# Second-layer weights as four neighbouring rows per partition, and last stores of 3, 6, 9 and 9 rows

## The chip, the cores and the metric

The kernel runs on one NeuronCore of one Trainium2 chip. The metric is the device time of one execution in microseconds (us). Before the change the median of three runs is 207.63 us (207.09 to 207.95).

## What is computed

Per batch and head (8 x 8, 576 positions, 64 dimensions) an attention over 32 pooled memory slots, and then a soft mixture of 8 experts over all 4608 rows of 512. The change touches only the experts and the output:

```python
    logits = x @ phi                       # x: 4608 x 512, phi: 512 x 32
    slot_input = d.T @ x                   # d: softmax of the logits over the rows
    for e in range(E):                     # 8 experts, 4 slots each
        h = np.maximum(slot_input[e] @ w1[e], 0.0)   # w1[e]: 512 x 1024
        slot_out[e] = h @ w2[e]                      # w2[e]: 1024 x 512
    return c @ slot_out                    # c: softmax of the logits over the 32 slots
```

All data are float32 in DRAM: 38 MB of q, k, v, 4.7 MB of phi, 16.8 MB each of w1 and w2, and an output of 9.4 MB.

## The kernel before, in words

The kernel writes no instruction directly. Each step is handed to a planner (`Plan.add`, L46) with its engine, a cost and the tiles that it reads and writes. The planner plays the program through with these costs and sets the order on each engine (`Plan.order`, L79). Loads and stores all go through the DMA queue of SyncE (SP), in planned order; each waits until the space that it fills, or the data that it sends, is free or ready.

The attention of the four pairs of batches runs first. Weights are loaded beside it, one half of a w1 matrix or of a w2 matrix (1 MB) at a time, into 20 slots of 2048 floats per partition (`ws`, L1258) and two more (`wqs`, L1260). A w1 half lands as two rows of 1024 floats per partition.

`expert_in` (L1323) is the first layer. For each expert and each half it issues 8 matmuls (L1332): the expert's 4 slots, with neighbours a weight block of 128 x 32, stand still, and 256 of the 1024 hidden units move through. The quarter `j` of the units goes to column tile `j` of TensorE (PE), so that quarter `j` of the hidden units ends on partitions 32j to 32j + 31 of the accumulator `hb`. `hidden` (L1343) applies the ReLU, splitting even and odd columns of `hb` apart, transposes both and scatters them to `hT`. So `hT` holds at partition p the units 256 j + 2 p + t, for j in 0 to 3 and t in 0 to 1.

`expert_out` (L1370) is the second layer. It needs row 256 j + 2 p + t of w2 at partition p, and so loads w2 as two neighbouring rows per partition and quarter: 256 contiguous pieces of 4 KB in each 1 MB load. Each half takes 16 matmuls of 128 x 32 by 256 (L1383), 8 for each half of the output columns, into `kvbank` and `scbank`. The very last megabyte is loaded in four parts of 256 KB (pieces of 1 KB).

Then `slot_sums` (L1304) copies both accumulators and adds the column tiles by matmul (L1316); L1499 and L1504 split the sums in two parts for the float32r format, and `out_mult` (L1510) multiplies the 32 slot outputs with the weights `c`. An output row here is one position of 9 per partition: the output is seen as 4 blocks `bp` of 128 partitions x 9 rows of 512. Each row of a block is a matmul pair (L1513), a copy from its accumulator bank by ScalarE (L1566) or VectorE (L1568) in turn, and its share of a store. The first three rows are stored one by one (L1546), the other 33 in 11 stores of three neighbouring rows (L1576): 6 KB in one piece per partition. They share 6 output tiles (`ots`, L1259), which lie over the weight slots, so a copy can have to wait for an earlier store.

Of the kernel before, what the change touches and what calls it, by code (L numbers as in the profile page):

```python
# [16 lines left out]
PE, DVE, ACT, POOL, SP = range(5)  # L17
# [3 lines left out]
class Plan:  # L21
# [24 lines left out]
    def add(self, eng, cost, fn, r=(), w=(), also=(), pri=None, dma=0.0, slack=0.0):  # L46
        cost, ni = cost if isinstance(cost, tuple) else (cost, 4)
        i = len(self.ops)
        deps = set()
        tiles = {}  # L50
        for x in r:
            for key in x:
                tiles[key[0]] = None
                if key in self.last_w:
                    deps.add(self.last_w[key])
        for x in w:
            for key in x:
                tiles[key[0]] = None
                if key in self.last_w:
                    deps.add(self.last_w[key])  # L60
                deps.update(self.reads.get(key, ()))
        for x in w:
            for key in x:
                self.last_w[key] = i
                self.reads[key] = []
        for x in r:
            for key in x:
                self.reads.setdefault(key, []).append(i)
        deps.discard(i)
        tiles = [t for t in tiles if t.pool is not None]  # L70
        for t in tiles:
            t.users += 1
        need = tiles + [t for t in also if t not in tiles]
        if pri is None:
            pri = self.phase[0]
            self.phase[0] += self.phase[1]
        self.ops.append((eng, cost, fn, deps, pri, dma, tiles, need, slack, ni))
# [170 lines left out]
def dve(n):  # L248
    return 0.15 + n / 960.0


def act(n, psum=True):
    return (0.16 if psum else 0.19) + n / 1200.0
# [15 lines left out]
def kernel(  # L269
# [24 lines left out]
    nc = tc.nc  # L294
    B, H, S, D = q.shape
    M = phi.shape[3]
    E, DM, FF = w1.shape
# [69 lines left out]
    def area(off, shape, n, below=(), fifo=False):  # L367

        size = shaped(off, shape)[1][1]
        xs = [shaped(off + i * size, shape) for i in range(n)]  # L370
        return Slots([a for a, _ in xs], [r for _, r in xs], below, fifo)
# [79 lines left out]
    def f():  # L451
        nc.vector.memset(ones, 1.0)
        for a in kps.aps:
            nc.vector.memset(a, 0.0)
        for a in sexs.aps:
            nc.vector.memset(a[:, PC:], 1.0)
        nc.vector.tensor_reduce(
            maskhp, ident.rearrange("p (c x) -> p c x", c=2), axis=AX.X, op=ALU.add
        )
        nc.vector.tensor_reduce(  # L460
            maskc, ident.rearrange("p (c x) -> p c x", c=C), axis=AX.X, op=ALU.add
        )
        nc.vector.tensor_reduce(
            rep[:, 0, :], ident.rearrange("p (a m) -> p m a", a=4), axis=AX.X, op=ALU.add
        )
        nc.vector.tensor_copy(rep[:, 1:4, :], rep[:, 0:1, :].to_broadcast([P, 3, NS]))
# [779 lines left out]
    def over(shape, n):  # L1246
# [10 lines left out]
    W0 = ARENA - NW * W_SZ  # L1257
    ws = area(W0, [W_SZ], NW, early)  # L1258
    ots = area(W0, [OT_SZ], NOUT, [ws])  # L1259
    wqs = Slots(  # L1260
        [qtile[:, i * W_SZ: i * W_SZ + W_SZ] for i in range(2)],
        [(TOP + i * W_SZ, W_SZ) for i in range(2)], [qs],
# [60 lines left out]
    def expert_in(e, hb):  # L1323
        w1v = w1[e].rearrange("(c p) f -> p c f", p=P)
        w1b = [load_w(w1v[:, 2 * i: 2 * i + 2], wqs if e == EG else ws) for i in range(2)]
        for i in range(2):

            def f(i=i):
                wv = w1b[i].ap.rearrange("p (c f) -> p c f", c=2)
                for c in range(2):  # L1330
                    for j in range(4):
                        nc.tensor.matmul(  # L1332
                            hb.ap[NS * j: NS * j + NS, :256],
                            SIM.ap[:, 2 * i + c, NS * e: NS * e + NS],
                            wv[:, c, 256 * j: 256 * j + 256],
                            start=(e % EG == 0 and i == 0 and c == 0),
                            stop=(e % EG == EG - 1 and i == 1 and c == 1),
                            tile_position=(0, NS * j),
                        )

            add(PE, (0.9, 32), f, r=[SIM, w1b[i]], w=[hb])
# [26 lines left out]
        )  # L1368

    def expert_out(e):  # L1370
        w2v = w2[e].rearrange("(j p t) d -> p j (t d)", j=4, t=2)
        w2h = w2[e].rearrange("(j p t) d -> p j t d", j=4, t=2)
        for i in range(2):
            last = e == E - 1 and i == 1
            t = ws.tile()
            wide = lambda t=t: t.ap.rearrange("p (j t d) -> p j t d", j=2, t=2)

            def mult(dst, d0, n, start, stop, i=i, wide=wide):
                for t in range(2):
                    for j in range(2):  # L1380

                        x = 2 * t + j
                        nc.tensor.matmul(  # L1383
                            dst[NS * x: NS * x + NS, :n],
                            hT()[:, 4 * t + 2 * i + j, NS * e: NS * e + NS],
                            wide()[:, j, t, d0: d0 + n],
                            start=start,
                            stop=stop,
                            tile_position=(0, NS * x),
                        )  # L1390

            if not last:
                load(
                    lambda t=t: t.ap.rearrange("p (a x) -> p a x", a=2),
                    w2v[:, 2 * i: 2 * i + 2], 1 << 20, t,
                )
                for d in range(2):
                    add(
                        PE, (0.5, 16),
                        lambda d=d, mult=mult, i=i: mult(  # L1400
                            pacc[d].ap[:, 0], d * HD, HD, e == 0 and i == 0, False
                        ),
                        r=[hTb.part(e // EG), t], w=[pacc[d]],
                    )
                continue
            t.split(4)
            for d in range(2):
                for j in range(2):
                    load(
                        lambda d=d, j=j: wide()[:, j, :, d * HD: d * HD + HD],  # L1410
                        w2h[:, 2 * i + j, :, d * HD: d * HD + HD], 1 << 18, t.part(2 * d + j),
                    )
            for d in range(2):
                add(
                    PE, (0.5, 16), lambda d=d, mult=mult: mult(pacc[d].ap[:, 0], d * HD, HD, False, True),
                    r=[hTb.part(e // EG), t.part(2 * d), t.part(2 * d + 1)], w=[pacc[d]],
                )
# [92 lines left out]
    def out_mult(bp, j, po, x):  # L1510
        y = HALF * (j % 2)
        for t in range(2):
            nc.tensor.matmul(  # L1513
                po.ap[:, : x.stop - x.start],
                cT[bp].ap[y: y + HALF, j // 2 * P: j // 2 * P + P],
                sr.ap[y: y + HALF, t, x],
                start=(t == 0),
                stop=(t == 1),
                tile_position=(y, 0),
            )  # L1520

    ot0 = ots.tile().split(2 * G)
    for d in range(2):
        x = slice(d * HD, d * HD + HD)
        for i in range(G):
# [17 lines left out]
            if d == 1:  # L1543
# [4 lines left out]
                    ),  # L1548
                    r=[ot0.part(2 * i), ot0.part(2 * i + 1)], dma=P * DM * 4 / DMA_RATE,
                )  # L1550
    for bp in range(NBP):
        for j0 in range(0 if bp else G, J, G):
            ot = ots.tile().split(G)
            for i in range(G):
                t = bp * J + j0 + i
                po = b_o.tile()
                add(
                    PE, 0.43,
                    lambda po=po, i=i, bp=bp, j0=j0: out_mult(bp, j0 + i, po, slice(0, DM)),
                    r=[sr, cT[bp]], w=[po], also=[ot],  # L1560
                )

                def f(po=po, ot=ot, i=i, t=t):
                    dst = ot.ap[:, i * DM: i * DM + DM]
                    if t % 2 == 0:
                        nc.scalar.copy(dst, po.ap[:, :DM])  # L1566
                    else:
                        nc.vector.tensor_copy(dst, po.ap[:, :DM])  # L1568

                add(  # L1570
                    *((ACT, act(DM)) if t % 2 == 0 else (DVE, dve(DM))), f,
                    r=[po], w=[ot.part(i)],
                )
            add(
                SP, 0.06,
                lambda bp=bp, j0=j0, ot=ot: nc.sync.dma_start(  # L1576
                    outv[bp * P: bp * P + P, j0: j0 + G, :],
                    ot.ap.rearrange("p (g d) -> p g d", g=G),
                ),
                r=[ot], dma=P * G * DM * 4 / DMA_RATE,  # L1580
            )

    with tc.manual_schedule():
        plan.issue()
# [28 lines left out]
```

## Time and profile before

| what | value |
|---|---|
| median of three runs | 207.63 us (207.09 to 207.95) |
| the profiled execution: its own time | 207.2 us |
| its span in the trace | 205.4 us |
| PE, DVE, ACT, POOL busy | 82%, 65%, 34%, 41% |
| HBM read and written | 66.65 MB, 9.44 MB |
| loads of weights, 1 MB each | 31, and 4 of 256 KB |
| output stores | 3 of 256 KB, 11 of 768 KB |

PE is TensorE, PEld its weight loads, DVE is VectorE, ACT ScalarE, POOL GpSimd, SP SyncE. `L1332` is a line of the kernel. In a table of stretches each row has the stretch from the span's start, its length, each engine's busy time with the count of instructions, PE's granted clock as a share, the DMA engines' mean busy share and the GB/s moved. In a table of groups stands: line, engine, operation, written tile and read tile with shapes, count, then busy us, mean ns of one, and the idle time before them with its releaser. In a timeline the idle time before an instruction and what ended it stand in brackets at the end. In the chain each row has start, duration, engine, tile and line.

### The profile page before, as it was taken

The numbers are of one execution on the slowest core, as the hardware profiler recorded it, in microseconds if no ns is written. First come the engines' busy times: TensorE is split into PE (matmuls) and PEld (weight loads), VectorE is DVE, ScalarE is ACT, GpSimd is POOL, SyncE is SP. The second block draws the span as 40 slices with busy tenths as digits, with TensorE's granted clock in tenths as the row PEclk, the third lists the DMA queues.
The fourth block names the chain that finished last, engine by engine and source line by source line (L and its number), as shares of the span: only waits on it lengthen the run. The fifth ranks groups of instructions, "written<-read, shape, count | busy, mean of one in ns | idle before, by whom it ended". The sixth has DMA issues, their size and how long they took to land.

```text
span 205.4 us, 5935 instructions
## 1 busy us (share of the span) xinstructions
PE 167.9 (82%) x2565; PEld 106.1 (52%) x2565; DVE 133.3 (65%) x232; ACT 69.8 (34%) x183; POOL 84.2 (41%) x84
## 2 busy tenths in 40 slices
PE   7999649978699899788999787989999957989400
PEld 6677534635366586455576364656555523545100
DVE  7822540899897999999899984672558400486500
ACT  2022405446541846436453430200113300475300
POOL 7199205689992995799834482000000000000000
PEclk9999996999979999999999999999999997899755
DMA  6999999999999999999999999999999995099994
GB/s 204 365 393 392 382 388 383 388 385 383 395 384 388 381 391 390 388 394 401 406 400 412 406 413 408 407 409 407 410 405 406 410 395 183 0 396 409 415 420 201
DMA packets 28986, 76.47 MB, mean 372 GB/s; under 512 B 1824, under 2 KB 6944, under 8 KB 28960
## 3 DMA queue, kind: packets, MB, share of 16 engines
q1 hardware_dynamic: 28960, 76.09, 96.9%
q8 instruction: 20, 0.33, 0.7%
q14 instruction: 6, 0.05, 0.1%
HBM read 66.65 MB, written 9.44 MB: 370 GB/s over the span
## 4 chain that ended last, share of the span: by engine, by line
PE 37%; DMA 21%; DVE 14%; POOL 11%; issue 4%; SPq 4%; ACT 2%; POOLq 1%; DVEq 1%; ACTq 0%
DMA arena<-in_moe_w_dram 9%; DMA arena<-in_v_dram 8%; PE bank L1332 7%; PE scbank L812 6%; PE kvbank L703 4%; PE bank L881 4%; SPq L501 4%; DMA out_dram<-arena 4%; POOL arena L847 3%; POOL arena L668 3%; PE bank L1513 3%; POOL arena L647 3%; POOL arena L870 2%; PE bank L1009 2%; DVE arena L605 2%
## 5 line engine op out<-in xcount | busy, mean ns | idle before, releaser
L647 POOL TENSOR_TENSOR arena<-arena 128x1152 f32<-128x1152 f32 x8 | 21.0, 2632 | 17.4 <-ACT arena L640 14.9
L590 DVE STREAM_TRANSPOSE arena<-top 128x1152 f32<-128x1152 f32 x16 | 21.6, 1353 | 8.2 <-DMA top<-in_q_dram 8.2
L703 PE MATMUL kvbank<-arena 64*32 64x128 f32 x1152 | 21.0, 277 | 6.2 <-issue 2.7
L812 PE MATMUL scbank<-arena 64*64 64x288 f32 x256 | 23.7, 447 | 2.3 <-DVE arena L826 2.3
L519 PE MATMUL kvbank<-ones 128*128 128x256 f32 x82 | 23.4, 422 | 2.4 <-ACT arena L727 1.3
L668 POOL TENSOR_TENSOR arena<-arena 128x128 f32<-128x128 f32 (+2 forms) x32 | 23.4, 730 | 3.2 <-ACT arena L656 1.3
L870 POOL TENSOR_TENSOR arena<-arena,ssm 128x576 f32<-128x576 f32 x16 | 18.3, 1151 | 9.6 <-DVE ssm L866 7.9
L703 PEld LDWEIGHTS kvbank<-arena 64*32 64x32 f32 x1152 | 16.5, 107 | 10.8 <-issue 5.6
L847 POOL TENSOR_TENSOR arena<-arena,smx 128x576 f32<-128x576 f32 x16 | 18.4, 1150 | 7.7 <-DVE smx L842 7.7
L881 PE MATMUL bank<-arena 128*128 128x288 f32 x64 | 18.7, 425 | 1.3 <-DVE arena L873 0.8
L605 DVE TENSOR_REDUCE arena<-arena 128x128 f32<-128x1152 f32 x8 | 17.2, 2155 | 3.9 <-DMA arena<-in_phi_dram 3.7
L519 PEld LDWEIGHTS kvbank<-ones 128*128 128x128 f32 x82 | 15.8, 207 | 6.0 <-ACT arena L727 1.7
L1513 PE MATMUL bank<-sr,cT 64*128 64x512 f32 (+1 forms) x78 | 14.7, 425 | 1.7 <-DVE arena L1568 1.3
L826 DVE STREAM_TRANSPOSE arena<-scbank 128x576 f32<-128x576 f32 x16 | 12.3, 766 | 5.6 <-PE scbank L812 5.5
L812 PEld LDWEIGHTS scbank<-arena 64*64 64x64 f32 x256 | 9.9, 141 | 10.2 <-DVE arena L826 3.7
L852 ACT ACTIVATE arena<-arena 128x576 f32<-128x576 f32 x16 | 10.9, 684 | 11.3 <-POOL arena L847 11.1
L881 PEld LDWEIGHTS bank<-arena 128*128 128x128 f32 x64 | 11.2, 189 | 6.4 <-DVE arena L873 2.1
L1383 PE MATMUL kvbank<-arena 128*32 128x256 f32 x128 | 10.8, 411 | 3.8 <-DMA arena<-in_moe_w_dram 3.8
L1568 DVE COPY arena<-bank 128x512 f32<-128x512 f32 x17 | 11.1, 688 | 4.2 <-PE bank L1513 2.5
L873 DVE STREAM_TRANSPOSE arena<-arena 128x576 f32<-128x576 f32 x16 | 11.9, 755 | 1.5 <-POOL arena L870 1.5
L1332 PE MATMUL bank<-arena,SIM 128*32 128x256 f32 x224 | 12.5, 379 | 0.4 <-DVE SIM L1232 0.4
L857 DVE TENSOR_REDUCE ssm<-arena 128x18 f32<-128x576 f32 x16 | 11.8, 738 | 1.0 <-ACT arena L852 0.7
(130 smaller groups left out, 238.4 us busy)
## 6 DMA issues: line engine op xcount, KB each, us to landing
arena<-in_moe_w_dram SPq DMA_DIRECT2D x29, 1024.0 KB, 15.3
top<-in_q_dram SPq DMA_DIRECT2D x8, 1152.0 KB, 12.6
arena<-in_k_dram SPq DMA_DIRECT2D x8, 1152.0 KB, 10.1
arena<-in_v_dram SPq DMA_DIRECT2D x8, 1152.0 KB, 12.5
out_dram<-arena SPq DMA_DIRECT2D x11, 768.0 KB, 8.7
arena<-in_phi_dram SPq DMA_DIRECT2D x8, 576.0 KB, 7.1
top<-in_moe_w_dram SPq DMA_DIRECT2D x2, 1024.0 KB, 11.1
arena<-in_moe_w_dram SPq DMA_DIRECT2D x4, 256.0 KB, 14.6
```

Source lines behind the costliest of these rows:

```text
L519: lambda: nc.tensor.matmul(warm.ap, ones, ones.unsqueeze(1).to_broadcast([P, 2, P]), start=True, stop=True,),
L590: lambda: nc.vector.transpose(qT.ap.rearrange("p (i u y) -> p u i y", i=2, y=Y), qt.ap[:, h * QT_SZ: h * QT_SZ + QT_SZ].rearrange("p (u i ...
L605: lambda: nc.vector.tensor_reduce(mx.ap[:, c0:c1], ph().rearrange("p c j m -> p c m j"), axis=AX.X, op=ALU.max),
L647: lambda: nc.gpsimd.tensor_tensor(ph(), ph(), mb.ap[:, c0:c1].unsqueeze(2).to_broadcast([P, c1 - c0, J, M]), op=ALU.subtract,),
L668: plus = lambda o, x, y: nc.gpsimd.tensor_tensor(o, x, y, op=ALU.add)
L703: nc.tensor.matmul(acc.ap[M * c: M * c + M, a, : 2 * D], ph()[h0: h0 + HALF, c, j, :], kv()[h0: h0 + HALF, :, c, j * D: j * D + D], start= ...
L812: nc.tensor.matmul(scb.ap[HALF * g: HALF * g + HALF, a, :JY], pair[g].kd.ap[h0: h0 + HALF, i, c].rearrange("p r m -> p (r m)"), pair[g].qT ...
L847: lambda: nc.gpsimd.tensor_tensor(exv(), exv(), bc(mx), op=ALU.subtract),
L870: lambda: nc.gpsimd.tensor_tensor(exv(), exv(), bc(sm), op=ALU.mult),
L881: nc.tensor.matmul(lp.ap[:, :JY], vpb.ap[:, h, :], aT.ap[:, a * JY: (a + 1) * JY], start=(h == 0), stop=(h == H - 1),)
L1332: nc.tensor.matmul(hb.ap[NS * j: NS * j + NS, :256], SIM.ap[:, 2 * i + c, NS * e: NS * e + NS], wv[:, c, 256 * j: 256 * j + 256], start=(e ...
L1513: nc.tensor.matmul(po.ap[:, : x.stop - x.start], cT[bp].ap[y: y + HALF, j // 2 * P: j // 2 * P + P], sr.ap[y: y + HALF, t, x], start=(t == 0),
```

## The change

Three edits, one of them in two places:

- **w2 loads.** Each half of w2[e] now goes to the partitions as four neighbouring rows (i p x: half, partition, row), so a 1 MB load has 128 contiguous pieces of 8 KB instead of 256 of 4 KB. The last megabyte keeps its four loads of 1 KB pieces, at other rows.
- **First-layer units.** `hT` must hold at partition p the units that belong to these rows, 512 i + 4 p + 2 j + t. So column tile j of the first layer now reads, out of a span of 512 units, the pairs 2 (j mod 2) and the one after it of every four: two floats, then a gap of two. The matmul count and shape are unchanged.
- **Last stores.** The 11 stores of three rows become three of 3 rows, one of 6 and two of 9 (12 and 18 KB in one piece per partition). The 6-row and the 9-row stores have tiles of their own beside the 6 of `ots`; no output tile is used twice any more.

```diff
     ots = area(W0, [OT_SZ], NOUT, [ws])
+    b0 = W0 + NOUT * OT_SZ
+    big = {6: area(b0, [6 * DM], 1, [ws]), 9: area(b0 + 6 * DM, [9 * DM], 2, [ws])}
...
-                            wv[:, c, 256 * j: 256 * j + 256],
+                            wv[:, c, 512 * (j // 2): 512 * (j // 2) + 512].rearrange(
+                                "p (x u t) -> p x u t", u=2, t=2
+                            )[:, :, j % 2, :],
...
-        w2v = w2[e].rearrange("(j p t) d -> p j (t d)", j=4, t=2)
-        w2h = w2[e].rearrange("(j p t) d -> p j t d", j=4, t=2)
+        w2v = w2[e].rearrange("(i p x) d -> p i (x d)", i=2, x=4)
+        w2h = w2[e].rearrange("(i p j t) d -> p i j t d", i=2, j=2, t=2)
...
-                    lambda t=t: t.ap.rearrange("p (a x) -> p a x", a=2),
-                    w2v[:, 2 * i: 2 * i + 2], 1 << 20, t,
+                    lambda t=t: t.ap, w2v[:, i], 1 << 20, t,
...
-    for bp in range(NBP):
-        for j0 in range(0 if bp else G, J, G):
-            ot = ots.tile().split(G)
-            for i in range(G):
+    for bp, j0, n in ((0, 3, 3), (0, 6, 3), *((1, 0, 3), (1, 3, 6), (2, 0, 9), (3, 0, 9))):
+        ot = (ots if n == G else big[n]).tile().split(n)
+        for i in range(n):
```

The rest of the last block is the same code with `n` in place of `G`.

The order of matmuls, copies and transposes is the same on every engine. On SyncE, this is the end of the weight loads before (`-`) and now (`+`); `in_moe_w_dram` is both w1 and w2, and a load's shape is that of its target in SBUF:

```order
 L501 DMA top<-in_moe_w_dram 128x2x1024
-L501 DMA arena<-in_moe_w_dram 128x2x1024 x19
+L501 DMA arena<-in_moe_w_dram 128x2x1024 x4
+L501 DMA arena<-in_moe_w_dram 128x2048 x15
 L501 DMA arena<-in_moe_w_dram 128x2x256 x4
```

The last 4 loads of w1 keep two pieces per partition; the 15 of w2 that follow have one of 2048 floats.

The end of SyncE's queue before, with what each store waits for (`DMAHW0` to `DMAHW7` are the counters of eight transfers under way, DVE and Activation the copies):

```order
L1576 DMA out_dram<-arena 128x1536 [waits DMAHW7_49,DVE_49,Activation_49]
L1576 DMA out_dram<-arena 128x1536 [waits DMAHW0_49,DVE_49,Activation_49]
L1576 DMA out_dram<-arena 128x1536 [waits DMAHW1_49,DVE_49,Activation_49]
L1576 DMA out_dram<-arena 128x1536 [waits DMAHW2_49,DVE_49,Activation_49]
L1576 DMA out_dram<-arena 128x1536 [waits DMAHW3_49,DVE_49,Activation_49]
L1576 DMA out_dram<-arena 128x1536 [waits DMAHW4_49,DVE_49,Activation_49]
```

And now:

```order
L1578 DMA out_dram<-arena 128x1536 [waits DMAHW7_49,DVE_49,Activation_49]
L1578 DMA out_dram<-arena 128x1536 [waits DMAHW0_49,DVE_49,Activation_49]
L1578 DMA out_dram<-arena 128x1536 [waits DMAHW1_49,DVE_49,Activation_49]
L1578 DMA out_dram<-arena 128x3072 [waits DMAHW2_49,DVE_49,Activation_49]
L1578 DMA out_dram<-arena 128x4608 [waits DMAHW3_49,DVE_49,Activation_49]
L1578 DMA out_dram<-arena 128x4608 [waits DMAHW4_49,DVE_49,Activation_49]
```

The first six stores after the three single rows were of 3 rows each and five more followed; now these six carry all 33 rows, and a store of 9 rows waits for nine copies.

More of the change, by code (lines that the diff above doesn't have):

```diff
@@ L1410, in expert_out @@
                         lambda d=d, j=j: wide()[:, j, :, d * HD: d * HD + HD],
-                        w2h[:, 2 * i + j, :, d * HD: d * HD + HD], 1 << 18, t.part(2 * d + j),
+                        w2h[:, i, j, :, d * HD: d * HD + HD], 1 << 18, t.part(2 * d + j),
                     )
@@ L1550 @@
                 )
-    for bp in range(NBP):
-        for j0 in range(0 if bp else G, J, G):
-            ot = ots.tile().split(G)
-            for i in range(G):
[L1555 to L1573, printed above, removed]
-            add(
[L1575 to L1580, printed above, removed]
-            )
@@ new lines, with f @@
+    for bp, j0, n in ((0, 3, 3), (0, 6, 3), *((1, 0, 3), (1, 3, 6), (2, 0, 9), (3, 0, 9))):
+        ot = (ots if n == G else big[n]).tile().split(n)
+        for i in range(n):
+            t = bp * J + j0 + i
+            po = b_o.tile()
+            add(
+                PE, 0.43,
+                lambda po=po, i=i, bp=bp, j0=j0: out_mult(bp, j0 + i, po, slice(0, DM)),
+                r=[sr, cT[bp]], w=[po], also=[ot],
+            )
+            def f(po=po, ot=ot, i=i, t=t):
+                dst = ot.ap[:, i * DM: i * DM + DM]
+                if t % 2 == 0:
+                    nc.scalar.copy(dst, po.ap[:, :DM])
+                else:
+                    nc.vector.tensor_copy(dst, po.ap[:, :DM])
+            add(
+                *((ACT, act(DM)) if t % 2 == 0 else (DVE, dve(DM))), f,
+                r=[po], w=[ot.part(i)],
+            )
+        add(
+            SP, 0.06,
+            lambda bp=bp, j0=j0, n=n, ot=ot: nc.sync.dma_start(
+                outv[bp * P: bp * P + P, j0: j0 + n, :],
+                ot.ap.rearrange("p (g d) -> p g d", g=n),
+            ),
+            r=[ot], dma=P * n * DM * 4 / DMA_RATE,
+        )
```

## The prediction

> **What bounds the kernel now.** I read the slices of the span first, then the chain of work that ended last, then stretches of single stages. The slices:
>
> ```profile
> PE   7999649978699899788999787989999957989400
> PEclk9999996999979999999999999999999997899755
> DMA  6999999999999999999999999999999995099994
> GB/s 204 365 393 392 382 388 383 388 385 383 395 384 388 381 391 390 388 394 401 406 400 412 406 413 408 407 409 407 410 405 406 410 395 183 0 396 409 415 420 201
> ```
>
> Each column is a fortieth of 205.4 us. The DMA engines are full except around slice 34, between the last weight and the first store. So the kernel is two full transfers with a gap: loads up to about 174 us, 4 us of compute, stores to the end. The end of the chain, in order of time:
>
> ```profile
> 136.70 7.98 PE bank L1332 x144
> ...
> 153.11 18.86 DMA arena<-in_moe_w_dram
> 172.02 0.96 PE kvbank L1383 x8
> 172.98 0.85 PE scbank L1383 x8
> 173.83 0.85 PE kvbank L1383 x8
> 174.69 1.08 PE scbank L1383 x8
> 175.77 0.64 PE bank L1316 x2
> ...
> 185.31 0.25 ACT arena L1566
> 185.55 7.75 DMA out_dram<-arena
> ```
>
> The second-layer matmuls (L1383) wait 18.86 us for weights; later the copies wait for stores. The last link is SyncE's wait for the last store:
>
> ```profile
> SPq L1608 <- DMA out_dram<-arena: 9.2, 1, 9.2
> ```
>
> The rate of each transfer stage, by the size of its pieces: 60 to 66 us holds k and q loads (pieces of 2,304 bytes), 110 to 165 weights (4,096), 184 to 202 three-row stores (6,144). Last column GB/s.
>
> ```profile
> core 0: us, PE busy (x) PEld busy (x) DVE busy (x) ACT busy (x) POOL busy (x), PEclk, DMA share, GB/s
> 60.00:66.00 6.00, 6.00 (x132) 4.32 (x135) 4.95 (x9) 1.00 (x3) 2.04 (x4) 1.00 1.05 389
> 110.00:165.00 55.00, 50.55 (x662) 29.88 (x665) 35.67 (x81) 12.92 (x41) 8.50 (x8) 1.00 1.03 408
> 184.00:202.00 18.00, 8.20 (x40) 4.50 (x38) 7.26 (x11) 5.56 (x10) 0.00 (x0) 0.74 1.02 416
> DMA packets 28986, 76.47 MB, mean 372 GB/s; under 512 B 1824, under 2 KB 6944, under 8 KB 28960
> ```
>
> Larger pieces go faster. The packet row tells that a piece is one packet up to 6 KB: between 2 and 8 KB it counts 28,960 - 6,944 = 22,016, which is 24 loads x 512 pieces of 2,304 bytes, 31 x 256 of 4,096, 3 x 128 of 2,048 and 11 x 128 of 6,144, unsplit.
>
> **The change, part by part.** *Price of a packet.* With 16 engines one packet takes 16 x bytes / rate: 94.8 ns for 2,304 bytes, 160.6 for 4,096, 236.3 for 6,144. From 4,096 to 6,144 that is 0.0370 ns a byte and 9.2 ns a packet; from 2,304 to 4,096 it is 0.0367 and 10.2. Loads and stores lie on one line, so I extend it, with 9.2 ns: 312 ns for 8,192 bytes, 463 for 12,288, 690 for 18,432. No row shows such packets; the bounds are 0 saved (the engine pays per 4 or 6 KB) and 10.2 ns a packet saved.
>
> [...]
>
> *Second-layer loads.* 15 loads of 1 MB become 128 packets of 8 KB instead of 256 of 4 KB: 8 fewer for each engine and load, 15 x 8 x 9.2 ns = 1.10 us. It is on the path, since DMA is full up to the last weight and PE waits for it. The last megabyte keeps its four loads of 1 KB pieces.
>
> *Stores.* Each engine has 88 packets of 6,144 bytes before, and afterwards 24 of those, 8 of 12,288 and 16 of 18,432: 48. 40 x 9.2 ns = 0.37 us, on the path as far as DMA never runs dry. That is the risk of a nine-row store: it waits for its ninth row. These rows give the pace and the start:
>
> ```profile
> 178.90 1.34 SPq L1546 DMA_DIRECT2D out_dram<-arena  x3
> ...
> 181.17 1.29 DVE L1568 COPY arena<-bank 128x512 f32<-128x512 f32 x2 [0.23 <-PE bank L1513]
> ...
> 182.68 1.29 DVE L1568 COPY arena<-bank 128x512 f32<-128x512 f32 x2 [0.22 <-PE bank L1513]
> 179.02:182.44 3.42, 3.00 (x20) 1.55 (x20) 2.93 (x5) 2.31 (x5) 0.00 (x0) 1.00 0.82 307
> ```
>
> VectorE finishes two rows every 1.51 us, ScalarE as many: 0.38 us a row. DMA takes 262,144 / 416e3 = 0.63 us a row. The 0.82 share says that DMA started 0.6 us into its stretch, near 179.7, 0.8 after the first issue. Twelve rows ahead of the six-row store keep it busy to 187.3; row 18 is done when the chain's store leaves, 185.55, and 0.8 more is 186.4: 0.9 us spare. The first nine-row store is needed at 191.1 and can start at 185.55 + 9 x 0.38 + 0.8 = 189.8: 1.3 spare; the last has over 3. The copies' waits for stores (every row now has its own place) were behind a full DMA, so losing them is worth nothing. Five fewer issues on SyncE also cost nothing: it has nothing else to do there.
>
> *First-layer matmuls.* The count stays 256; only the moving operand's steps change, two floats of every four over a span of 512. The before rate, and the nearest rows for a strided or a longer read:
>
> ```profile
> 136.70:144.50 7.80, 7.80 (x144) 4.57 (x144) 1.00 1.02 406
> L605 DVE TENSOR_REDUCE arena<-arena 128x128 f32<-128x1152 f32 x8 | 17.2, 2155 | 3.9 <-DMA arena<-in_phi_dram 3.7
> L842 DVE TENSOR_REDUCE smx<-arena 128x18 f32<-128x576 f32 x16 | 11.8, 737 | 0.4
> ```
>
> 54.2 ns a matmul, 13.9 us in all (x256). VectorE's reduction over single floats 128 bytes apart takes 1.87 ns an element, the contiguous one 1.28: a factor of 1.46. If PE had to sweep the whole span it would be 2. No row excludes either, nor 1; I take 1, because pairs of adjacent floats are nearer to the contiguous row than single ones 128 bytes apart. What hides a lesser cost is the time that PE waits for weights afterwards:
>
> ```profile
> 166.90 0.64 PE L1383 MATMUL kvbank<-arena 128*32 128x256 f32 x8 [0.81 <-DMA arena<-in_moe_w_dram]
> 169.50 0.64 PE L1383 MATMUL kvbank<-arena 128*32 128x256 f32 x8 [1.52 <-DMA arena<-in_moe_w_dram]
> 172.02 0.96 PE L1383 MATMUL kvbank<-arena 128*32 128x256 f32 x8 [1.45 <-DMA arena<-in_moe_w_dram]
> ```
>
> 3.8 us, less the 1.1 by which loads come earlier: 2.7 us, a factor of 1.19, is free.
>
> [...]
>
> *Sum.* 1.10 + 0.37 = 1.47, 1.48 before rounding. The profiled execution took 207.2 us (its span of 205.4 and 1.8 around it), which gives 205.7; the median of the three runs, 207.63, lies 0.4 above it, which gives 206.15. I forecast 206.2. A difference of 0.5% (1.04 us) is about what a measurement of this kernel can tell from none.
>
> **The rivals.** *The half-clock stretch goes, too.* PE's clock is granted in stretches of 3.41 us; those followed by half clock, and their nearest exceptions:
>
> ```profile
> 25.42:28.83 3.41, 1.94 (x116) 1.67 (x117) 1.17 (x1) 0.51 (x2) 0.00 (x0) 1.00 1.07 387
> 28.83:32.25 3.42, 1.23 (x33) 0.72 (x32) 1.22 (x2) 0.95 (x4) 0.00 (x0) 1.00 1.05 387
> 52.73:56.14 3.41, 1.75 (x13) 1.23 (x13) 3.19 (x7) 2.29 (x8) 3.41 (x3) 1.00 1.04 397
> 165.37:168.78 3.41, 1.79 (x32) 0.56 (x23) 0.00 (x0) 0.00 (x0) 0.00 (x0) 1.00 1.03 395
> 168.78:172.20 3.42, 1.25 (x20) 0.57 (x24) 0.00 (x0) 0.00 (x0) 0.00 (x0) 1.00 0.77 279
> 172.20:175.61 3.41, 3.41 (x32) 1.48 (x24) 0.42 (x1) 0.00 (x0) 0.00 (x0) 0.50 0.20 69
> ```
>
> Busy for 1.23, 1.75 and 1.25 us was followed by half clock, 1.79 and 1.94 was not. With weights 1.1 us earlier, two tiles fall into 168.78 to 172.20 and PE is busy for about 1.8: a toss. At full clock the last weights' matmuls and the sums after them end some 0.85 us sooner (half of 0.85 + 0.85): 205.3. Against it: the gate can close one stretch later.
>
> *No gain above 4 KB.* If the price goes by bytes beyond some size, or the rate by the row of 416 GB/s at best, little is left: 207.2 to 207.6, no change. For it, only that no row lies above 6 KB; against it, that three sizes lie on a line.
>
> [...]
>
> *Slower: the stepped read holds PE.* Place: the first-layer matmuls, 136.7 to 151 us. A factor r costs 13.9 x (r - 1); 2.7 us are hidden, 1.5 are paid by the change's gain, and about 2.0 more come back because a PE that never waits would not fall to half clock (0.96 + 0.85 + 0.85 + 1.08 = 3.74 us at half against 1.7 at full). So it decides from r = 1.45. At 1.46 the time is 207.8, at 2 it is 207.63 + 13.9 - 6.2 = 215.3. For it: four column tiles read at once, at 54 ns a matmul. Against it: only half of each 16 bytes is skipped.
>
> *Stores run dry.* If rows came at 0.65 us instead of 0.38, above the 0.53 at which the first nine-row store is late (191.1 - 0.8 - 185.55 over 9 rows), that store would start 1.1 us late: 207.3.
>
> **How the numbers follow.** The forecast has 0.37 (its own range 205.6 to 206.9), the half clock gone 0.20, no gain above 4 KB 0.18, the stepped read 0.18, dry stores 0.07. Faster by over 0.5% (below 206.6): 0.29 of the forecast, 0.20, and 0.01 of the last, 0.50. Slower (above 208.7): 0.14 of the stepped read, 0.02 of no gain and 0.01 of the last, 0.17. Within: the rest, 0.33. The range of 205.0 to 208.0 leaves out the stepped read's upper part and a little below.
>
> **What would show it.** Right: second-layer loads at about 420 GB/s, stores at 420 to 428, first-layer matmuls still near 54 ns each, first store near 177.8 us, no gap in DMA between stores. Wrong: 408 GB/s with 8 KB packets (no gain above 4 KB); first-layer matmuls past 151 us and no wait of L1383's successors for weights (stepped read); DMA share under 1 near 187 or 191 us (dry stores).

## The result, and the profile after

The changed kernel took 205.84 us in the median of 4 runs (205.65 to 206.26), the kernel before 207.58 beside it (207.09 to 207.95): a ratio of 0.9938, 95% interval 0.991 to 0.9965. Measured a second time (a1 below) it was 205.85 against 206.94, 0.9942 (0.9926 to 0.9957). The forecast was 206.2. The profiled execution took 206.26 us, with a span of 204.5.

The slices of the changed kernel, and its packets:

```profile
PEclk9999995799999999999999999999999997999755
DMA  6999999999999999999999999999999994099994
GB/s 203 366 390 394 380 388 384 386 386 382 383 387 388 383 388 392 388 394 398 407 389 417 405 410 409 412 426 418 420 415 420 418 410 172 0 395 423 447 404 180
DMA packets 26346, 76.47 MB, mean 374 GB/s; under 512 B 1744, under 2 KB 6864, under 8 KB 24016
...
q8 instruction: 20, 0.33, 0.7%
```

The picture is the same: full, a gap, full. Packets of 2 to 8 KB are now 24,016 - 6,864 = 17,152, which is 24 x 512 + 16 x 256 + 3 x 128 + 3 x 128; so the 15 loads of 8 KB pieces and the three large stores are still one packet for each piece: the 26,346 - 24,016 = 2,330 larger ones are 15 x 128, 3 x 128 and 26 packets of instructions. The last row names a queue that the prediction passed over. It comes back below.

Stretches of single stages (columns as in the prediction), the second of them w2 loads alone:

```profile
60.00:66.00 6.00, 6.00 (x133) 4.08 (x130) 5.72 (x10) 1.07 (x4) 3.24 (x5) 1.00 1.05 390
...
135.00:160.00 25.00, 24.18 (x378) 13.83 (x378) 14.69 (x38) 3.70 (x11) 0.00 (x0) 1.00 1.01 418
184.00:198.00 14.00, 6.74 (x36) 3.42 (x34) 6.58 (x11) 5.21 (x10) 0.00 (x0) 0.78 1.01 425
```

The k and q loads, untouched, run at the old rate. The w2 loads went up to 418 GB/s, the stores to 425. The same 25 us of the kernel before, and of experiment e4 with 2 KB pieces:

```profile
135.00:160.00 25.00, 24.43 (x393) 13.96 (x397) 15.02 (x38) 4.58 (x15) 0.00 (x0) 1.00 1.03 407
```

```profile
135.00:160.00 25.00, 24.33 (x384) 13.79 (x383) 15.09 (x38) 3.69 (x11) 0.00 (x0) 1.00 1.05 387
```

At 16 engines an 8 KB packet takes 16 x 8,192 / 418e3 = 313.6 ns where two of 4 KB take 2 x 161.0: 8.4 ns saved for each packet less. Two of 2 KB take 2 x 84.7 where one of 4 KB takes 161.0: again 8.4 ns. One price, 8.4 ns, fits from 2 to 8 KB.

The path through the end of the loads, in the chain, then PE's last waits for weights and the first store in the timeline:

```profile
138.19 13.42 DMA arena<-in_moe_w_dram
151.68 19.68 DMA arena<-in_moe_w_dram
171.40 1.08 PE kvbank L1387 x8
```

```profile
168.91 0.64 PE L1387 MATMUL kvbank<-arena 128*32 128x256 f32 x8 [0.81 <-DMA arena<-in_moe_w_dram]
...
171.40 1.08 PE L1387 MATMUL kvbank<-arena 128*32 128x256 f32 x8 [1.42 <-DMA arena<-in_moe_w_dram]
...
178.11 1.34 SPq L1549 DMA_DIRECT2D out_dram<-arena  x3
```

PE still waits for weights, 2.2 us in all where it was 3.8 (0.81, 1.52 and 1.45): loads that come earlier and a slower first-layer read have used up the rest. The first store leaves at 178.11 instead of 178.90. The end, in stretches of 1 us, of the kernel before and of the changed one:

```profile
201.00:202.00 1.00, 0.00 (x0) 0.00 (x0) 0.00 (x0) 0.00 (x0) 0.00 (x0) 0.50 0.98 406
202.00:203.00 1.00, 0.00 (x0) 0.00 (x0) 0.00 (x0) 0.00 (x0) 0.00 (x0) 0.50 0.74 301
203.00:204.00 1.00, 0.00 (x0) 0.00 (x0) 0.00 (x0) 0.00 (x0) 0.00 (x0) 0.50 0.06 25
```

```profile
201.00:202.00 1.00, 0.00 (x0) 0.00 (x0) 0.00 (x0) 0.00 (x0) 0.00 (x0) 0.50 0.09 37
202.00:203.00 1.00, 0.00 (x0) 0.00 (x0) 0.00 (x0) 0.00 (x0) 0.00 (x0) 0.50 0.04 18
```

One engine of 16 alone is a share of 0.06, and both kernels end near it: 0.06 before, 0.09 and 0.04 in the changed kernel. There the last store has landed on 15 engines by 202.03, and one works on alone; it lands there 1.6 us after it has landed on the first engine (table below).

For the experiments I worked out from the trace when each load and store has landed on the first and on the last of the 16 engines, and when the last instruction transfer (the queue of 20 packets above, 16 KB each) started. In every one of these executions the last store lands on 15 engines within 0.24 us of each other; only the sixteenth is later in some, by up to 2.1 us behind the first (e2). Times in us of the profiled execution; "per load" is the mean over 15 w2 loads on the engine that lands first:

| kernel | per load | first store issued | last instruction transfer | end, first engine | end, last engine |
|---|---|---|---|---|---|
| before | 2.550 | 178.90 | 181.7 | 203.08 | 204.38 |
| e3, first-layer read alone | 2.554 | 178.54 | 180.9 | 202.70 | 204.29 |
| e2, stores alone | 2.551 | 178.80 | 180.9 | 202.54 | 204.67 |
| e1, loads alone | 2.484 | 177.90 | 179.5 | 202.06 | 202.91 |
| changed kernel | 2.488 | 178.11 | 179.8 | 201.84 | 203.46 |
| a1, the same again | 2.484 | 177.80 | 179.4 | 201.53 | 202.78 |
| e7, stores 3, 3, 9, 9, 9 | 2.482 | 177.81 | 179.4 | 202.19 | 202.88 |
| e6, 16 more PE instructions, late | 2.485 | 177.26 | 178.0 | 201.78 | 202.25 |
| e8, 16 more PE instructions, early | 2.482 | 177.84 | 178.2 | 202.49 | 202.69 |
| e9, 44 more | 2.484 | 177.65 | 175.3 | 201.39 | 201.57 |
| e10, 44 more, old stores | 2.483 | 177.96 | 175.8 | 202.13 | 202.29 |
| e11, 44 more, stores 3, 3, 9, 9, 9 | 2.481 | 179.20 | 177.2 | 203.57 | 203.76 |

### The profile page after: what moved, and what is told of

It is laid out like the page before. It is cut to its first block, busy times and chain, and to the rows that moved or that the text cites. A ratio compares the mean times of both kernels' runs of the same rounds, so it can differ in the third digit from the quotient of the medians.

```text
span 204.5 us, 5914 instructions
## 1 busy us (share of the span) xinstructions
PE 166.9 (82%) x2565; PEld 105.8 (52%) x2565; DVE 132.9 (65%) x232; ACT 70.3 (34%) x183; POOL 84.3 (41%) x84
## 2 busy tenths in 40 slices
DMA packets 26346, 76.47 MB, mean 374 GB/s; under 512 B 1744, under 2 KB 6864, under 8 KB 24016
## 4 chain that ended last, share of the span: by engine, by line
DMA 29%; PE 28%; POOL 15%; DVE 10%; issue 5%; SPq 4%; ACT 2%; POOLq 1%; DVEq 0%; ACTq 0%
DMA arena<-in_moe_w_dram 16%; DMA arena<-in_v_dram 8%; PE bank L1516 6%; POOL arena L668 4%; POOL arena L847 4%; DMA arena<-in_phi_dram 4%; PE scbank L812 4%; PE bank L881 4%; SPq L501 4%; PE kvbank L703 4%; POOL arena L870 4%; POOL arena L647 3%; DVE arena L1570 2%; PE bank L1009 2%; DVE arena L605 1%
## 5 line engine op out<-in xcount | busy, mean ns | idle before, releaser
L812 PE MATMUL scbank<-arena 64*64 64x288 f32 x256 | 23.1, 436 | 1.9 <-DVE arena L826 1.9
L1516 PE MATMUL bank<-sr,cT 64*128 64x512 f32 (+1 forms) x78 | 14.0, 422 | 0.8 <-DVE arena L1570 0.6
L852 ACT ACTIVATE arena<-arena 128x576 f32<-128x576 f32 x16 | 10.9, 684 | 10.2 <-POOL arena L847 9.9
L1334 PE MATMUL bank<-arena,SIM 128*32 128x256 f32 x224 | 13.2, 390 | 0.4 <-DVE SIM L1232 0.4
L1387 PE MATMUL kvbank<-arena 128*32 128x256 f32 x128 | 10.9, 415 | 2.2 <-DMA arena<-in_moe_w_dram 2.2
L857 DVE TENSOR_REDUCE ssm<-arena 128x18 f32<-128x576 f32 x16 | 11.8, 736 | 0.9 <-ACT arena L852 0.8
```

Source lines behind the costliest of these rows:

```text
L812: nc.tensor.matmul(scb.ap[HALF * g: HALF * g + HALF, a, :JY], pair[g].kd.ap[h0: h0 + HALF, i, c].rearrange("p r m -> p (r m)"), pair[g].qT ...
L1516: nc.tensor.matmul(po.ap[:, : x.stop - x.start], cT[bp].ap[y: y + HALF, j // 2 * P: j // 2 * P + P], sr.ap[y: y + HALF, t, x], start=(t == 0),
```

## The experiments

The theory: packets cost about 9 ns each, loads and stores both gain by it, and the first-layer read is free. The rivals: no gain above 4 KB, a stepped read with a price that shows, a half-clock stretch that goes, stores that run dry.

### The parts by themselves: e1, e2, e3

e1 is the changed kernel with the store loop of before:

```diff
-    for bp, j0, n in ((0, 3, 3), (0, 6, 3), *((1, 0, 3), (1, 3, 6), (2, 0, 9), (3, 0, 9))):
-        ot = (ots if n == G else big[n]).tile().split(n)
+    for bp in range(NBP):
+        for j0 in range(0 if bp else G, J, G):
+            ot = ots.tile().split(G)
...
```

> Second-layer loads of 8 KB pieces with the stepped first-layer read; the eleven three-row stores stay. Theory (a packet costs about 9 ns beside its bytes, loads are on the path, the stepped read is hidden): 15 loads at 2.49 us each instead of 2.55, so 0.9 to 1.1 us less than before, near 206.5. Rival (the gain came from the copies and stores, or from the half-clock stretch): within 0.3 us of before, 207.3 to 207.9.

Measured: 206.04 us (7 runs) against 207.31, 0.9933 (0.9909 to 0.9958). At 207.3 that is 1.39 us, 0.87 to 1.89. A w2 load took 2.484 us instead of 2.550, so 15 of them came 0.99 us earlier, and the first store left 1.0 us earlier. As far as the intervals can tell, loads alone bring all of the gain that the whole change shows.

e2 is the changed kernel with the loads and the first-layer read of before:

```diff
-                            wv[:, c, 512 * (j // 2): 512 * (j // 2) + 512].rearrange(
-                                "p (x u t) -> p x u t", u=2, t=2
-                            )[:, :, j % 2, :],
+                            wv[:, c, 256 * j: 256 * j + 256],
...
-        w2v = w2[e].rearrange("(i p x) d -> p i (x d)", i=2, x=4)
+        w2v = w2[e].rearrange("(j p t) d -> p j (t d)", j=4, t=2)
...
```

> The stores of 3, 6, 9 and 9 rows alone, loads and first layer as before. Theory: 40 packets fewer for each engine, 0.3 to 0.5 us less than before, near 207.2, DMA without a gap between stores. Rival (a nine-row store lets DMA run dry, or large packets gain nothing): 207.6 or more.

Measured: 206.84 us (12 runs), 0.9987 (0.9966 to 1.0008): from 0.70 us gained to 0.17 lost. The 0.37 of the forecast is inside, and so is nothing. The table says more: from first store to end the first engine took 23.74 us instead of 24.18, the last 25.87 instead of 25.48. The engine that ends last gained nothing in this execution; its instruction packet took 1.66 us, and 0.93 in the kernel before.

e3 is the kernel before with the stepped read:

```diff
-                            wv[:, c, 256 * j: 256 * j + 256],
+                            wv[:, c, 512 * (j // 2): 512 * (j // 2) + 512].rearrange(
+                                "p (x u t) -> p x u t", u=2, t=2
+                            )[:, :, j % 2, :],
```

> The stepped first-layer read alone, loads and stores as before; it leaves the pairing of hidden units with second-layer rows undone, so only its time counts. Theory: first-layer matmuls at about 57 ns each instead of 54 (0.7 us in all), hidden by the wait for weights: within 0.3 us of before. Rival (the read is on the path): 0.7 us or more above before.

Measured: 207.14 us (12 runs), 0.9998 (0.9976 to 1.0021). It costs nothing that shows at the end, but it isn't free on PE. The matmuls of this line, first in the kernel before, then in e3 (duration shortest/median/longest, start of the first and the last):

```profile
L1332 PE MATMUL bank<-arena,SIM x224: 378/379/404, 136.7 to 150.8; 128*32 128x256 f32 x112
```

```profile
L1332 PE MATMUL bank<-arena,SIM x224: 385/388/413, 136.8 to 151.7; 128*32 128x256 f32 x112
```

The stage takes 14.9 us instead of 14.1, a factor of 1.06; PE waits for weights behind it anyway.

### Sizes pushed the other way: e4, e5

e4 is the kernel before with w2 in pieces of one row, 2 KB:

```diff
-                hb.ap[:, :256].rearrange("p (x t) -> p t x", t=2), AF.Relu,
+                hb.ap[:, :256].rearrange("p (t x) -> p t x", t=2), AF.Relu,
...
-        w2v = w2[e].rearrange("(j p t) d -> p j (t d)", j=4, t=2)
+        w2v = w2[e].rearrange("(j t p) d -> p j t d", j=4, t=2)
...
```

> The other way: second-layer loads of 15 x 1 MB in pieces of 2 KB, stores as before, first-layer read as before. Theory (9.2 ns a packet): 32 packets of 85 ns for each engine and load, 2.72 us instead of 2.57, 2.2 us in all: 209.8. Rival (time goes by bytes): 207.6.

Measured: 209.47 us (6 runs), 1.0105 (1.0073 to 1.0137), so 2.18 us slower at 207.3, with 387 GB/s in the stretch shown above. Its loads have 15 x 16 more packets an engine: 2.18 / 240 is 9.1 ns each, 6.3 to 11.8 by the interval. The price of a packet holds in the time as well as in the rate, in both directions.

e5 is the kernel before with the first layer reading every fourth float:

```diff
-                            wv[:, c, 256 * j: 256 * j + 256],
+                            wv[:, c].rearrange("p (x u) -> p x u", u=4)[:, :, j],
```

> On the kernel before, the first layer reads single floats, every fourth of 1024, so that no two come from the same 16 bytes; it pairs hidden units with other rows of the second layer, so only its time counts. Theory (reading two of four floats is just enough, one of four is not): a first-layer matmul takes 1.5 to 2 times its 54 ns, 7 to 14 us more, of which 3.8 us are hidden: 208 to 216. Rival (steps cost little on this path): 55 to 60 ns a matmul and 207.6.

Measured: 217.23 us (4 runs), 1.0491 (1.0462 to 1.0519), 10.2 us slower. Its matmuls, and then the stretch that they fill:

```profile
L1332 PE MATMUL bank<-arena,SIM x224: 617/632/671, 136.9 to 166.0; 128*32 128x256 f32 x112
```

```profile
137.00:166.00 29.00, 29.00 (x254) 9.92 (x258) 8.17 (x18) 1.27 (x3) 0.00 (x0) 1.00 1.03 408
```

29.0 us for 254 matmuls is 114 ns each, 2.1 times 54.2; both that and the time lie above what was expected. So the danger in the prediction's slow rival was real, one step from the pattern that was used: one float of four doubled the stage (a factor of 2.1), two neighbours of four cost a twentieth (1.06). The way its price was worked out held, too: 13.9 x 1.1 = 15.3 us, less 3.8 of waits and 2.0 for a PE that does not fall to half clock (in e5 the clock is 1.00 from 165.37 to 179.02 us), is 9.5, with 10.2 measured.

### The changed kernel again, and the dry store: a1, e7

a1 is the changed kernel without an edit, measured once more.

> The changed kernel once more, beside the next three. Theory: 205.8 to 206.2, 1.2 to 1.7 us below before.

Measured: 205.85 us (6 runs) against 206.94, 0.9942 (0.9926 to 0.9957). PE's clock differs between the two profiled executions. The stretch around the last weights in the first:

```profile
168.78:172.20 3.42, 1.87 (x24) 0.81 (x28) 0.00 (x0) 0.00 (x0) 0.00 (x0) 0.87 0.64 228
172.20:175.61 3.41, 3.41 (x31) 1.51 (x24) 0.42 (x1) 0.37 (x1) 0.00 (x0) 0.63 0.07 24
```

and in a1:

```profile
167.92:171.33 3.41, 1.25 (x20) 0.42 (x16) 0.00 (x0) 0.00 (x0) 0.00 (x0) 1.00 0.75 268
171.33:174.75 3.42, 3.33 (x33) 1.23 (x34) 0.42 (x1) 0.02 (x1) 0.00 (x0) 1.00 0.16 55
```

Half clock came in the one and not in the other. The first store left 178.11 - 173.99 = 4.12 us after the last weight in the first and 177.80 - 174.00 = 3.80 in a1. So the stretch is worth 0.3 us here. It isn't tied to the change: e3, with the loads of before, had none either (178.54 - 174.74 = 3.80).

e7 makes the store after the two of three rows wait for nine:

```diff
-    big = {6: area(b0, [6 * DM], 1, [ws]), 9: area(b0 + 6 * DM, [9 * DM], 2, [ws])}
+    big = {9: area(b0, [9 * DM], 3, [ws])}
...
-    for bp, j0, n in ((0, 3, 3), (0, 6, 3), *((1, 0, 3), (1, 3, 6), (2, 0, 9), (3, 0, 9))):
+    for bp, j0, n in ((0, 3, 3), (0, 6, 3), (1, 0, 9), (2, 0, 9), (3, 0, 9)):
```

> The changed kernel with the last stores of 3, 3, 9, 9 and 9 rows. Theory: row 18 is ready near 184.8 us and its packets 0.85 later, but DMA has sent the first nine rows near 184.9: 0.75 us dry, less 0.07 for 8 packets fewer, so 206.5 and a gap in DMA near 185. Rival (rows are ahead anyway): 205.8.

Measured: 205.64 us (6 runs), 0.9928 (0.9912 to 0.9944). The hole is there, first the changed kernel, then e7:

```profile
184.00:190.00 6.00, 5.96 (x34) 3.13 (x32) 5.13 (x9) 4.54 (x9) 0.00 (x0) 1.00 1.01 418
```

```profile
184.50:185.50 1.00, 1.00 (x8) 0.70 (x8) 0.90 (x2) 0.74 (x2) 0.00 (x0) 1.00 0.73 307
...
184.00:190.00 6.00, 5.85 (x34) 3.09 (x34) 5.23 (x9) 4.80 (x9) 0.00 (x0) 1.00 0.91 382
```

A share of 0.91 over 6 us, 0.10 less, is 0.6 us without work, and yet the time did not grow to the 206.5 that was expected. The table tells why: the first engine ends 0.66 us later than in a1, but the last one only 0.10. It used the hole to catch up: its lag behind the first went from 1.59 us ahead of the first nine-row store to 0.81 behind it. The other engines have time to spare at the end, the first 0.69 us.

### The engine that ends last: e6, e8, e9, e10, e11

e6 was made for the clock: four idle matmuls behind the 13th and the 14th w2 tile, to keep PE busy in the stretches before the last weights.

```diff
+    KEEP = {12: 1, 13: 3}
+
+    def keep_warm(n):
+        for _ in range(n):
+            nc.tensor.matmul(
+                warm.ap, ones, ones.unsqueeze(1).to_broadcast([P, 2, P]), start=True, stop=True,
+            )
...
```

> The changed kernel with four idle matmuls on ones (0.42 us each) in PE's last waits for weights, one after the 13th and three after the 14th tile of 1 MB. Theory (the half clock from 172 to 175.6 us is on the path): full clock there, the last matmuls and the sums end 0.85 us sooner, 205.0; if the half clock comes one stretch later instead, 205.4 to 205.8. Rival (the last landing sets the end anyway): no change, 205.8.

Measured: 205.41 us (6 runs), 0.9927 (0.9906 to 0.9947). Faster than a1 by 0.4 us at the median, but a1's profile had full clock (1.00 in the rows above) without it. e8 puts the same four matmuls behind the first w2 tile, 15 us earlier (L1387 starts at 152.16 us in the timeline, the 13th tile's at 167.05), so not in those stretches:

```diff
+    EXTRA = {0: 4}
...
```

> The changed kernel with the same four idle matmuls as the run that kept PE busy, but behind the first second-layer tile near 152 us, where PE is behind and the later wait for weights hides them. Theory A (there the gain came from the place of PE's 16 KB instruction transfer, which comes at a fixed instruction count and delays one DMA engine in the store stage): also 205.4, the transfer near 178 us. Theory B (it came from the clock): 205.85, as the changed kernel.

Measured: 205.41 us (6 runs) against 207.13, 0.9921 (0.9892 to 0.995). The same time as e6, so what e6 gained needs no busy PE at that place. Against a1 both gain 0.4 us at the median, but the intervals of the ratios overlap, and the profiled executions do not give one reason for it. In e6 the last weight landed 0.54 us earlier than in a1 (173.46 and 174.00 on the last engine), and the stores took as long there (24.99 and 24.98). In e8 the last engine ended 0.20 us behind the first instead of 1.25; but SyncE took 1.54 us to issue the second store instead of 0.38, its first landing came 1.0 us later (181.35 and 180.34), and the end only 0.09 earlier. So these two runs do not show what the lag costs.

What both share is 16 more PE instructions (2,573 matmuls and 2,573 weight loads on the page instead of 2,565), and that moves the instruction transfers: the last one starts at 178.0 and 178.2 us instead of 179.4 in a1. In the kernel before and in the changed one, the packet near 128 us starts behind the same 1,876 matmuls and 1,876 weight loads. PE's 5,130 instructions and the 20 packets fit one packet for 256 in the mean, an estimate from these two totals. A packet is 16 KB (20 in 0.33 MB), and where it fell among the stores, one engine was late. The last of these packets starts at 179.8 us in the changed kernel, among the first stores. The DMA queues in 178 to 182 us, of the changed kernel (packets, MB, share of 16 engines):

```profile
q1 hardware_dynamic: 478, 1.13, 74.0%
q8 instruction: 1, 0.02, 2.3%
```

2.3% of 16 x 4 us is 1.5 us on one engine, which then has its share of all later stores still to do. The landings show the step: the first store lands on all 16 engines within 0.18 us, the second on 15 within 0.19 and on the last 2.18 us after the first. e9 moves the packet out of the stores, with one small matmul behind each of the first 11 w2 tiles, 44 more PE instructions:

```diff
+    EXTRA = {x: 1 for x in range(11)}
...
+                warm.ap[:, :128], ones, ones[:, :128], start=True, stop=True,
...
```

> The changed kernel with eleven small idle matmuls (128 columns), one behind each of the first eleven second-layer tiles, 44 PE instructions more ahead of the stores. Theory A: the 16 KB instruction transfer moves from near 179.5 us to near 176, where DMA is idle; no engine lags in the store stage, the end comes 0.7 to 1.2 us sooner: 204.7 to 205.2. Rival (the lag does not set the end, or PE stalls for the transfer): 205.85 or more.

Measured: 204.96 us (12 runs), 0.992 (0.9889 to 0.9951). Eight runs lie at 204.41 to 205.00, four at 206.03 to 207.44. The packet in 174 to 178 us, where no load and no store is on its way, and the end:

```profile
q8 instruction: 1, 0.02, 1.4%
```

```profile
200.00:201.00 1.00, 0.00 (x0) 0.00 (x0) 0.00 (x0) 0.00 (x0) 0.00 (x0) 0.50 0.69 295
201.00:202.00 1.00, 0.00 (x0) 0.00 (x0) 0.00 (x0) 0.00 (x0) 0.00 (x0) 0.50 0.01 0
```

The tail of one engine is gone: the first engine ends at 201.39, the last at 201.57. e10 is e9 with the old stores:

> The same eleven matmuls with the stores of three rows. Theory A: with no lagging engine the saving of the larger stores shows in full, so this is 0.45 us above the run with the large stores, 205.1 to 205.7. Rival (large stores save nothing): equal to it.

Measured: 205.03 us (6 runs, 204.75 to 205.10), 0.9903 (0.9875 to 0.9931). Against e1, which is the same but for the place of the packet, all of its runs are lower (e1: 205.61 to 206.32; the two were not measured side by side, and the kernel before took 207.13 beside e10, 207.31 beside e1). In the profiled executions the first store leaves at the same time (177.96 and 177.90), the first engine takes as long from there (24.17 and 24.16 us), and the last one 24.33 instead of 25.01. So the lag is worth 0.7 us in these two, and moving the packet removes it. And e9 against e10 is the change of the stores with the tail out of the way: from first store to end 23.92 us instead of 24.33, 0.41 less, where 0.37 was forecast. In the medians of all runs, 204.96 and 205.03, the difference can't be seen for e9's scatter; e9's eight lower runs have 204.83.

e11 is e9 with the stores of e7:

> The same eleven matmuls with last stores of 3, 3, 9, 9 and 9 rows. Theory A: the 0.65 us for which DMA is dry near 185 us were hidden behind the lagging engine; without it they show: 0.5 to 0.6 us above the run with stores of 3, 6, 9 and 9 rows. Rival (they are made up in another way): equal to it.

Measured: 206.0 us (12 runs; six at 205.27 to 205.53, six at 206.47 to 207.48), 0.9949 (0.992 to 0.9979). Now the hole costs what it should. Two stretches of e11, and after them the same of e9:

```profile
186.00:187.00 1.00, 1.00 (x6) 0.67 (x8) 0.99 (x2) 0.69 (x3) 0.00 (x0) 1.00 0.69 295
187.00:188.00 1.00, 1.00 (x8) 0.59 (x6) 0.79 (x2) 0.98 (x2) 0.00 (x0) 1.00 0.69 295
```

```profile
186.00:187.00 1.00, 1.00 (x6) 0.63 (x7) 1.00 (x2) 0.78 (x2) 0.00 (x0) 1.00 1.18 498
187.00:188.00 1.00, 1.00 (x8) 0.44 (x6) 0.78 (x2) 0.87 (x2) 0.00 (x0) 1.00 0.94 393
```

From first store to end it took 24.56 us instead of 23.92, 0.64 more; the lower groups of runs, 205.34 and 204.83, differ by 0.5.

The scatter of e9 and e11 has a likely reason. Their higher runs have a mean granted clock of 0.942 to 0.951, the lower ones 0.955 to 0.969. One more stretch of 3.41 us at half clock takes 3.41 / 2 / 203 = 0.008 off that mean, so it would be one or two stretches. The profiled execution of e11 is a higher run (206.63 us), that of e9 the lowest (204.41), and up to the stores the two kernels are the same. In e11's, PE ran at half clock from 30.67 to 37.50 and from 57.98 to 61.39 us, three stretches; in e9's only from 43.33 to 46.74. The last weight landed at the same time (173.80 and 173.84), but in e11 PE was still behind, with no wait for weights, and the first store left 5.40 us after that weight instead of 3.81. By this reading the 11 small matmuls, 0.42 us each, have used up PE's waits, and time lost early reaches the end. That is one profile of each kind; whether the other higher runs are like it is open. e10's six runs, with a clock of 0.955 to 0.969, have no such group.

## Why the prediction was right, and where it was not

- **What bounds it.** Right. Two full transfers with a gap; shorter loads moved the first store, and the end followed. But the prediction takes the 16 DMA engines as one, and each transfer ends on its last engine.
- **Price of a packet.** Right: 9.2 ns by the line through three rates; 8.4 to 9.1 by e4 and the rate above 4 KB. The large stores lie on the same line: on the first engine of the changed kernel they land at 187.13, 190.83, 196.35 and 201.84 us, eight packets apart, so a packet of 12,288 bytes takes 462 ns and one of 18,432 takes 690 and 686, where the line gave 463 and 690. The rival without a gain above 4 KB is out: 418 GB/s at 8 KB, and 425 in the stores where the kernel before has 415 (184 to 198 us).
- **Second-layer loads, 1.10 us.** Right in kind; 0.99 on the engine that lands first. The last weight came 0.68 us earlier on the engine that lands last (174.67 to 173.99), and the first store 0.79, in a1 1.10. e1's whole time is 1.39 less, with 0.87 at the low end. In its profiled execution the end came 1.47 us earlier: 1.00 with the first store, and 0.47 because the last engine took 25.01 us for the stores instead of 25.48, with the first engine unchanged (24.16 and 24.18). That second part goes with the instruction packet, at 179.5 us instead of 181.7, and is not in the prediction.
- **Stores, 0.37 us.** The step that failed: "on the path as far as DMA never runs dry". DMA did not run dry, and 15 engines saved 0.45 us (23.73 instead of 24.18 from first store to the first engine's end). But the path ends on the engine that got the last instruction packet. On it the changed kernel took 25.35 us from first store to end, before 25.48; a1 24.98, and e1 with the old stores 25.01. Against e1 nothing is left. The lag itself tells more: from the third store to the last it shrinks from 2.00 us to 1.30 in the kernel before, over 88 packets, and from 2.08 to 1.62 in the changed kernel, over 48, so by 8.0 and 9.6 ns a packet. By this the late engine is faster by about the price of a packet that the others pay, and has nothing to gain from fewer packets. That is an estimate from two profiles, and why it is faster no run shows. With the instruction packet elsewhere (e9, e10) the term is 0.41.
- **First-layer matmuls at no cost.** Not quite: 57 ns each (7.48 us for 132) instead of 54.2. The cover that was named, the waits for weights, held it; e3 is 0.9998 of before.
- **The half clock.** The toss was well called, the price not: 0.85 us was forecast, from matmuls and sums both at half rate, and 0.3 was measured between the changed kernel's two profiles (4.12 and 3.80 us from last weight to first store). It comes and goes between executions of kernels with the old loads as well (0.50 from 172.20 to 175.61 us in the kernel before, 1.00 in e3), so it is no effect of the change.
- **Dry stores.** Right: no hole in the changed kernel. e7 and e11 made one of the size that the pace of rows gives.
- **The sum.** 1.48 was forecast; the ratios give 0.0062 and 0.0058 of 207.3, 1.3 and 1.2, and their intervals (0.7 to 1.9, 0.9 to 1.5) hold 1.48. The lost store term and a load term at or above its forecast both lie within that, so the total can't tell them apart; the store stage's rows do. That the total is so near is in part luck: the 0.37 of the stores did not reach the end as it was worked out, and yet the last engine's store stage was shorter, by 0.13 us in the changed kernel's first profile and 0.50 in a1, as it was by 0.47 in e1, which has the old stores. That goes with where the instruction packet fell.

The row for the stretch in which those 57 ns stand, of the changed kernel's first-layer matmuls alone (PE, PEld, clock, DMA share, GB/s):

```profile
137.00:144.50 7.50, 7.48 (x132) 4.47 (x136) 1.00 1.02 421
```

The best version is the changed kernel with the 11 small matmuls (e9, 204.96 us, 0.992) or the same with the old stores (e10, 205.03, 0.9903). Their lead over the changed kernel rests on the tail that goes; the intervals of the ratios overlap, and e9 scatters.

## What to carry to other kernels

Where DMA is full, count packets: take the price of one from the rates of the stages that the kernel already has (8.4 to 9.2 ns here), and check that the stage ends on all 16 engines together. A stage that ends on a DMA share of 0.06 ends on one engine, and what helps the other 15 does not shorten it (e2: 0.44 us less on the first engine, none on the last); look for what else that engine carries. A read with gaps cost a twentieth here where it took two neighbouring floats of every four (14.9 us for the stage instead of 14.1), and doubled the stage where it took one (114 ns a matmul instead of 54.2); price it against the wait behind it.

## What the runs showed that was not expected

- Instructions came in 20 packets of 16 KB, each on one of the engines that move the data; by the totals that is one for 256 of PE's 5,130 instructions, an estimate. The last one took 0.9 (e9) to 1.7 us (e2). Where it fell among the stores, its engine ended later than the others, by 1.6 us in the changed kernel (201.84 and 203.46) and 2.1 in e2. 44 idle PE instructions moved the last packet from 179.8 to 175.3 us, into the gap, and the two ends to 0.18 us of each other.
- The loads carry more of this than the stores. In the kernel before, the engines on which a load lands over 1.5 us after the first are one after the first packet (19.7 us), two after the second (28.1), three after the third (34.4), four after the next (42.3) and five after the one at 48.6: by these counts, each of these packets went to another engine. In the changed kernel the last weight landed on the first engine at 169.72 us and on the last at 173.99. No run was made to close these 4.3 us.
- So a kernel can get faster by instructions that compute nothing: e10, 44 more than e1, took 205.03 us against 206.04.
- Two neighbouring floats of each four cost TensorE 5 to 6% with four column tiles (14.9 us for the stage instead of 14.1), one of four 110% (114 ns a matmul instead of 54.2).
